# Decode attention and gated MLP on one core: eight megabytes of weights moved from SyncE's DMA queue to the head of ScalarE's

## The chip, the cores and the metric

The kernel runs on one core of one Trainium2 chip. The metric is the device time of one execution in microseconds (us). A core has five engines with an instruction stream each: TensorE (PE in the profile; its weight loads are PEld), VectorE (DVE), ScalarE (ACT), GpSimd (POOL) and SyncE (SP). Each stream runs strictly in its order; streams wait for each other on semaphores. DMAs are issued from SyncE's stream (SPq) and ScalarE's (ACTq); sixteen DMA engines move the data.

## What is computed

Two layers, each an attention block and a gated block with residuals, for 4 batches of one token (bf16). Both layers use the same weights and the same caches.

```python
def A(x, k_cache, v_cache, wq, wo):            # x: 4 x 1 x 512
    q = (x @ wq).reshape(B, Sq, 32, 128)       # 32 query heads, 8 key/value heads
    scores = einsum(q, k) * 128 ** -0.5        # caches: 4 x 8 x 4096 x 128
    return (softmax(scores) @ v) @ wo          # wo: 4096 x 512
def B(x, w_gate, w_up, w_down):                # 512 x 1792, 512 x 1792, 1792 x 512
    return (sigmoid(x @ w_gate) * (x @ w_up)) @ w_down
x = x + A(layernorm(x), ...);  x = x + B(layernorm(x), ...)
x = x + A(layernorm(x), ...);  x = x + B(layernorm(x), ...)
```

The caches and weights are 114.56 MB as they are read by this kernel (half of the heads' tiles are read a second time for the second layer).

## The kernel before

**Work.** A unit is one (batch, head group, layer), written `bhl`: unit 010 is batch 0, second group of four key/value heads, layer 0. The 16 units run in the order `000 010 100 011 110 200 001 111 ...` (UNITS, line 30). A unit of fresh tiles takes eight K tiles and eight V tiles of 512 KB. K tiles are transposed on VectorE (L723) and multiplied by the queries on TensorE (L731, `unit_scores`); softmax follows (`unit_probs`, L754 to L798), with its exponential and a copy on ScalarE; V tiles are multiplied by the probabilities (L815, `unit_values`), the result is copied by ScalarE (L827), selected (L832), scaled (L839) and multiplied by w_o (L850), which is added to x (L862). When both groups of a batch in layer 0 are done, `chain` runs its gated layer: mean and variance (L872 to L902), gate and up matmuls (L912), tanh on ScalarE (L932), product and transpose on VectorE (L937, L944), down matmuls (L954), x (L977) and the next layer's norm. Units with group 1 and layer 1 (011, 111, ...) use the tiles of group 1, layer 0, which stay in SBUF until then.

**Tiles.** K and V tiles live in a ring of 23 slots. A tile's load waits until the users of the slot's previous tile are done.

**Weights.** They have places of their own in SBUF and wait for nothing: w_q in two halves (wq0 for head group 0, wq1 for group 1; `load_wq`), w_o in four quarters (wo0 to wo3; `load_wo`), and w_gate, w_up, w_down (`load_glu`); all are issued at L519. Each has a semaphore of its own. One row that a DMA moves is 4,096 bytes of w_q, of a K or of a V tile, 3,584 of w_gate and w_up, 2,048 of w_down, 1,024 of w_o.

**What sets the order.** All loads are issued by SyncE in the order of the string LOADS (line 31):

```python
LOADS = "wq0 K0000 K0001 K0002 K0003 wq1 K0100 V0000 K0101 V0001 K0102 V0002 K0103 V0003
 wo0 wo1 wo2 wo3 K1000 K1001 K1002 K1003 V0100 V0101 V0102 V0103 wg wu wd V1000 ... V1003
 K1100 ... K1103 K2000 ... K2003 K0010 V1100 ..."          # each K or V word: two tiles
```

So the first 24 tiles are K of unit 000, then K of 010 and V of 000 in turn; then K of 100, V of 010, the weights of the gated layer, V of 100. `_Plan.schedule` plans all engines with a cost for each operation and a model of the loads, assigns slots, and writes each engine's order into `S.prog`. It also puts filler matmuls (L1105), which compute nothing that is used, where TensorE would stand idle by the plan; they keep their place in TensorE's order whatever happens on the chip. `emit` then writes each engine's stream from `S.prog`, with the waits. In the plan the tanh L932 waits for w_down as well as for its own inputs. TensorE's order around batch 0's gated layer is: the values of unit 010, its w_o, norm, gate, 13 fillers, up, 15 fillers, 4 fillers behind tanh, half of down, two value matmul groups of unit 100, the other half of down, the next norm, the queries of unit 011 mixed with more values of unit 100, the scores of unit 011.

In ScalarE's order the load of x (L447) is first; its first computation is `maskrs` (L695), ahead of it the table load, then the copy of the queries (L630).

The lines that emit the streams, and where the change is put:

```python
    S.schedule()
    with nc.Block() as block:
        for name, starter in (("sp", block.sync), ("act", block.scalar), ...):
            def body(e, name=name):
                S.emit(name, e, sems)
```

Of the kernel before, what the change touches and what calls it, by code (L numbers as in the profile page):

```python
# [350 lines left out]
def bass_interleave_layers__gqa_block_cached__glu_gated_glu__decode_kernel(nc, A_x, A_k, A_v, A_wq, A_wo, B_x, B_wg, B_wu, B_wd, out):  # L351
# [23 lines left out]
    S = _Plan(SLOTS)  # L375
# [3 lines left out]
    def sb(name, shape, dtype=dt.float32):  # L379
        return es.enter_context(nc.sbuf_tensor(name, list(shape), dtype))  # L380
# [8 lines left out]
    wg = sb("wg", [P, KD, F], bf)  # L389
    wu = sb("wu", [P, KD, F], bf)  # L390
    wd = sb("wd", [P, FB, D], bf)
# [713 lines left out]
    S.filler(lambda e: e.matmul(PT_ps[:, 0:256], lhsT=ident, rhs=flat_even[:, 0:256], start=True, stop=True), "PT")  # L1105

    S.schedule()
    with nc.Block() as block:
        for name, starter in (
            ("sp", block.sync), ("act", block.scalar), ("pe", block.tensor), ("dve", block.vector),  # L1110
            ("pool", block.gpsimd),
        ):
            def body(e, name=name):
                S.emit(name, e, sems)

            starter(body)
# [29 lines left out]
```

## Time and profile before

| what | value |
|---|---|
| runs shown | 314.67, 314.79 and 310.01 us, median 314.67 |
| profiled execution | 312.2 us; its span from first to last instruction 310.5 us |
| PE, PEld, DVE, ACT, POOL busy | 213.2, 114.2, 168.1, 60.8, 12.6 us |
| q1 (the loads) | 114.57 MB, 94.6% of sixteen engines' span |
| DMAs by SyncE | 96 K tiles, 96 V tiles, 2 of w_q, 4 of w_o, w_gate, w_up, w_down |
| TensorE's granted clock, mean | 0.899 |

How to read it: the slices of the page cut the span into 40 parts of 7.76 us; a digit is the busy share in tenths. A timeline line gives start, duration, engine, source line, operation, output <- inputs, shape and count, and in brackets the idle time just before it with what ended it. For SPq and ACTq lines the duration is that of the issuing instruction with its waits merged in; the landing of the data is shown as "us to landing" in the DMA view.

### The profile page before, as it was taken

The page shows a single profiled execution, that of the slowest core. Times are in us where ns is not written, and L with a number is a line of the kernel's source. Part 1 is how long each engine was busy: PE and PEld are TensorE (multiplying, and loading weights), DVE is VectorE, ACT ScalarE, POOL GpSimd, SP SyncE. Part 2 cuts the span into 40 slices and gives each one's busy share as a digit, 9 for nine tenths or more (in the row PEclk, how much of TensorE's full clock was granted, in tenths as well). Part 3 has the DMA queues.
Part 4 walks back from the last instruction along what each step waited for, and adds up shares of the span by engine and source line. Part 5 has one row for each costly group of instructions (what it writes and reads, how often), then busy time and mean ns, then how long its engine had stood idle before and what let it go on. Part 6 is the DMA issues. An engine that isn't in the chain of part 4 may idle for free.

```text
span 310.5 us, 7729 instructions
## 1 busy us (share of the span) xinstructions
PE 213.2 (69%) x3395; PEld 114.2 (37%) x3395; DVE 168.1 (54%) x314; ACT 60.8 (20%) x151; POOL 12.6 (4%) x44
## 2 busy tenths in 40 slices
PE   1344446577838976776996866885974757788694
PEld 1213114433425632243553422462431424534243
DVE  3675542483001699596217863736996952475112
ACT  0202002002101312021323120131330213231301
POOL 8000000000000000000000000000000000000001
PEclk9999999959995998599978877997897999979859
DMA  7999999999999999999999999799999999999900
GB/s 265 411 408 410 409 388 348 395 410 409 404 397 411 402 409 407 407 411 395 380 413 385 409 410 406 283 340 408 331 414 410 408 401 373 394 352 411 391 9 4
DMA packets 34931, 115.09 MB, mean 371 GB/s; under 512 B 3280, under 2 KB 7376, under 8 KB 34896
## 3 DMA queue, kind: packets, MB, share of 16 engines
q1 hardware_dynamic: 34832, 114.57, 94.6%
q8 instruction: 27, 0.44, 0.6%
q14 instruction: 8, 0.07, 0.1%
q10 hardware_dynamic: 64, 0.01, 0.0%
HBM read 114.56 MB, written 0.00 MB: 369 GB/s over the span
## 4 chain that ended last, share of the span: by engine, by line
DMA 57%; PE 25%; DVE 8%; SPq 4%; issue 3%; ACT 3%; POOL 1%; DVEq 0%; ACTq 0%
DMA ring<-in_A_k_cache_dram 20%; DMA ring<-in_A_v_cache_dram 17%; DMA wd<-in_B_w_down_dram 7%; PE S_ps L731 7%; DMA wq<-in_A_wq_dram 6%; DMA wo<-in_A_wo_dram 5%; PE O_ps L815 5%; DVE ring L723 4%; SPq L514 3%; PE M_ps L850 2%; PE Q_ps L651 2%; PE G_ps L954 1%; PE PT_ps L1105 1%; SPq L519 1%; PE PT_ps L779 1%
## 5 line engine op out<-in xcount | busy, mean ns | idle before, releaser
L723 DVE STREAM_TRANSPOSE ring<-ring 128x1024 int32<-128x1024 int32 x96 | 116.1, 1227 | 33.4 <-DMA ring<-in_A_k_cache_dram 32.6
L731 PE MATMUL S_ps<-ring,qz 128*32 128x512 bf16 x512 | 48.4, 505 | 32.7 <-DVE ring L723 26.0
L815 PE MATMUL O_ps<-ring,pt_sb 128*16 128x512 bf16 x512 | 45.4, 442 | 20.5 <-DMA ring<-in_A_v_cache_dram 17.5
L1105 PE MATMUL PT_ps<-even 128*128 128x256 bf16 x305 | 50.5, 305 | 8.9 <-ACT pp L932 4.3
L1105 PEld LDWEIGHTS PT_ps<-even 128*128 128x128 bf16 x305 | 29.1, 109 | 27.5 <-issue 9.8
L827 ACT ACTIVATE b<-O_ps 128x512 bf16<-128x512 f32 x32 | 19.1, 596 | 85.3 <-PE O_ps L815 81.8
L731 PEld LDWEIGHTS S_ps<-ring,qz 128*32 128x32 bf16 x512 | 13.9, 113 | 55.5 <-DVE ring L723 31.5
L768 ACT ACTIVATE pp<-S_ps,tr 128x512 bf16<-128x512 f32 x16 | 13.2, 828 | 50.4 <-DVE tr L761 48.5
L754 DVE TENSOR_REDUCE stat<-S_ps 128x1 f32<-128x512 f32 x16 | 11.1, 692 | 21.9 <-PE S_ps L731 21.8
L815 PEld LDWEIGHTS O_ps<-ring,pt_sb 128*16 128x16 bf16 x512 | 9.7, 89 | 32.8 <-issue 13.1
L850 PE MATMUL M_ps<-oT,wo 128*128 128x32 bf16 x512 | 15.8, 178 | 2.0 <-DMA wo<-in_A_wo_dram 1.6
L839 DVE TENSOR_TENSOR oT<-M_ps,rl 128x8 bf16<-128x8 f32 x32 | 4.9, 152 | 22.7 <-PE M_ps L832 22.7
L850 PEld LDWEIGHTS M_ps<-oT,wo 128*128 128x128 bf16 x512 | 14.1, 97 | 7.3 <-DVE oT L839 2.9
L902 POOL TENSOR_TENSOR stat<-stat 128x1 f32<-128x1 f32 x8 | 4.4, 545 | 256.2 <-ACT stat L898 256.2
L789 ACT ACTIVATE pt_sb<-PT_ps 128x512 bf16<-128x512 f32 x16 | 9.6, 597 | 17.6 <-PE PT_ps L779 17.6
L832 PE MATMUL M_ps<-sel_o,b 128*128 128x32 bf16 x128 | 8.7, 183 | 4.7 <-ACT b L827 4.6
L832 PEld LDWEIGHTS M_ps<-sel_o,b 128*128 128x128 bf16 x128 | 5.8, 101 | 16.1 <-ACT b L827 12.3
L937 DVE SCALAR_TENSOR_TENSOR b<-pp,U_ps 128x448 bf16<-128x448 f32 (+2 forms) x6 | 3.2, 538 | 14.5 <-ACT pp L932 12.9
L695 ACT ACTIVATE maskrs<-mask,stat 128x16 f32<-128x16 f32 x16 | 4.5, 304 | 28.5 <-DVE qz L700 26.5
L793 PE MATMUL M_ps<-sel_h,stat 128*128 128x16 f32 x32 | 6.7, 286 | 4.4 <-ACT pp L768 4.1
L774 DVE STREAM_TRANSPOSE pp<-pp 128x256 int32<-128x256 int32 x16 | 6.8, 426 | 5.2 <-ACT pp L768 5.2
L700 DVE TENSOR_TENSOR qz<-Q_ps,maskrs 128x256 bf16<-128x256 f32 x16 | 6.3, 394 | 6.0 <-PE Q_ps L690 6.0
(112 smaller groups left out, 162.6 us busy)
## 6 DMA issues: line engine op xcount, KB each, us to landing
ring<-in_A_k_cache_dram SPq DMA_DIRECT2D x96, 512.0 KB, 9.7
ring<-in_A_v_cache_dram SPq DMA_DIRECT2D x96, 512.0 KB, 10.2
wq<-in_A_wq_dram SPq DMA_DIRECT2D x2, 2048.0 KB, 13.8
wo<-in_A_wo_dram SPq DMA_DIRECT2D x4, 1024.0 KB, 14.7
wg<-in_B_w_gate_dram SPq DMA_DIRECT2D x1, 1792.0 KB, 16.1
wu<-in_B_w_up_dram SPq DMA_DIRECT2D x1, 1792.0 KB, 20.2
wd<-in_B_w_down_dram SPq DMA_DIRECT2D x1, 1792.0 KB, 22.7
xin<-in_A_x_dram ACTq DMA_DIRECT2D x1, 4.0 KB, 3.4
```

What stands on the lines that cost most here:

```text
L514: S.put("sp", lambda e: e.dma_start(ring[t.slot], src), dma="ring", load=t, size=0.524, cost=0.5)
L723: "dve", lambda e, t=t: e.transpose(ring[t.slot].bitcast(dt.int32), ring[t.slot].bitcast(dt.int32)),
L731: fns.append(lambda e, s=s, t=t, nn=nn, q=q: e.matmul(S_ps[qi][32 * s:32 * s + 32, :], lhsT=window(qi, s * NQ + nn, q), rhs=ring[t.slot].r ...
L754: dve(lambda e: e.tensor_reduce(ml[at], bank, AX.X, ALU.max, negate=True), keys(f"S{qi}", ss), keys("ml", ss), 0.7)
L768: lambda e: e.activation(p_sb[at].rearrange("p (t j r) -> p t r j", j=32, r=2), bank.rearrange("p (t r j) -> p t r j", r=2, j=32), ACTF.Ex ...
L774: dve(lambda e: e.transpose(pd[at].bitcast(dt.int32), p_sb[at].bitcast(dt.int32)), [own("P")], [own("P") + "d"], 0.4)
L789: "act", lambda e: e.activation(pt_sb[qi][:, cols], PT_ps[:, cols], ACTF.Copy),
L815: fns.append(lambda e, m=m, at=at, v=v, c=c, q=q: e.matmul(O_ps[m:m + 16, :], lhsT=pt[:, at:at + 16], rhs=ring[v.slot][:, c * 512:(c + 1) ...
L827: "act", lambda e: e.activation(b1[:], O_ps[:], ACTF.Copy),
L832: fns.append(lambda e, tt=tt: e.matmul(M_ps[:, 0:WIDE], lhsT=b1[:, tt * P:(tt + 1) * P], rhs=sel_o[:, tt, :].unsqueeze(1).broadcast_to([P, ...
L850: fns.append(lambda e, k=k, n=n, h0=h0: e.matmul(M_ps[:, k * WIDE:(k + 1) * WIDE], lhsT=wo[:, h0 + n, k * P:(k + 1) * P], rhs=oT[:, b, h0 ...
L1105: S.filler(lambda e: e.matmul(PT_ps[:, 0:256], lhsT=ident, rhs=flat_even[:, 0:256], start=True, stop=True), "PT")
```

## The change

After planning, the DMAs of wq1, w_gate, w_up, w_down and wo0 are taken out of SyncE's stream and put into ScalarE's, right behind the load of x and ahead of all its computation, in that order. Nothing else changes: the orders of the other engines, the slots of the ring, the fillers and all waits stay as planned. SyncE then issues wq0, the 24 tiles without wq1 among them, wo1 to wo3, K of 100, V of 010, V of 100 and so on without weights in between.

```diff
     S.schedule()
+
+    beside = [op for key in ("wq1", "wg", "wu", "wd", "wo0") for op in S.prog["sp"] if op.sem == key]
+    S.prog["sp"] = [op for op in S.prog["sp"] if op not in beside]
+    S.prog["act"][1:1] = beside
     with nc.Block() as block:
```

## The prediction

> **What bounds the kernel now.** I read the page's forty slices first, for the resource that is never idle.
>
> ```profile
> DVE  3675542483001699596217863736996952475112
> DMA  7999999999999999999999999799999999999900
> GB/s 265 411 408 410 409 388 348 395 410 409 404 397 411 402 409 407 407 411 395 380 413 385 409 410 406 283 340 408 331 414 410 408 401 373 394 352 411 391 9 4
> ```
>
> The DMA engines are full from the first slice to the 38th at about 410 GB/s; VectorE and TensorE are not. At that rate a 512 KB tile takes 512 KiB / 410 GB/s = 1.28 us. Time is lost only where the rate dips (slices 24 to 34) and in the tail. So the question is whether the change moves fewer bytes (no), moves them at another rate, or opens or closes a gap. The only early place where a weight ends a wait is batch 0's gated layer. The timeline of SyncE gives the issues around it:
>
> ```profile
> 66.03 0.33 SPq L514 DMA_DIRECT2D ring<-in_A_v_cache_dram  x1
> 66.40 0.43 SPq L519 DMA_DIRECT2D wg<-in_B_w_gate_dram  x1
> 66.88 2.54 SPq L519 DMA_DIRECT2D wu<-in_B_w_up_dram  x1
> 69.46 0.51 SPq L519 DMA_DIRECT2D wd<-in_B_w_down_dram  x1
> ...
> 95.94 0.33 SPq L514 DMA_DIRECT2D ring<-in_A_v_cache_dram  x1
> ```
>
> The first is the last V tile of unit 010; the DMA view gives it 12.0 us to landing, so it lands at 78.1. w_down takes 22.7 us and lands at 92.1. The timeline of all engines shows the layer running in the shadow of the weights:
>
> ```profile
> 78.12 0.61 PE L815 MATMUL O_ps<-ring,pt_sb 128*16 128x512 bf16 x8 [0.83 <-DMA ring<-in_A_v_cache_dram]
> 81.75 0.23 DVE L876 TENSOR_SCALAR small<-x,U_ps 128x4 bf16<-128x4 f32 x1 [0.55 <-PE U_ps L872]
> 82.67 0.74 PE L912 MATMUL G_ps<-wg,small 128*1 128x448 bf16 x12 [0.69 <-DMA wg<-in_B_w_gate_dram]
> 83.94 1.59 PE L1105 MATMUL PT_ps<-even 128*128 128x256 bf16 x13
> 87.11 0.93 PE L912 MATMUL U_ps<-wu,small 128*1 128x448 bf16 x16 [1.57 <-DMA wu<-in_B_w_up_dram]
> 87.97 1.81 PE L1105 MATMUL PT_ps<-even 128*128 128x256 bf16 x15
> 92.22 0.64 ACT L932 ACTIVATE pp<-G_ps,stat 128x448 f32<-128x448 f32 x1 [8.29 <-DMA wd<-in_B_w_down_dram]
> 92.91 0.61 PE L1105 MATMUL PT_ps<-even 128*128 128x256 bf16 x4 [3.13 <-ACT pp L932]
> 94.01 0.93 PE L954 MATMUL G_ps<-pp,wd 128*128 128x32 bf16 x28 [0.49 <-DVE pp L944]
> 94.86 1.03 PE L815 MATMUL O_ps<-ring,pt_sb 128*16 128x512 bf16 x8
> ```
>
> See that attention's end, norm, gate and up all run between 78 and 88 while weights land; only tanh onwards is left for after 92.1, and the down matmuls start at 94.0, 1.9 us behind the last weight. See also 13 + 15 + 4 L1105 filler matmuls, written into TensorE's order here to keep it busy during that wait. Behind them stand unit 100's value matmuls (94.86), which free the slots that SyncE waits for at 95.94.
>
> **Part 1: the bytes are kept, their order is not.** Nothing is added: 2.10 (w_q half) + 3 x 1.84 + 1.05 (w_o quarter) = 8.65 MB move to the second queue. SyncE's five issues go away; they cost it 0.43 to 2.54 us each, hidden since its tiles wait some 10 us in the queue (the page's medians, 9.7 and 10.2 us to landing). In the kernel before, 92.1 is when everything up to w_down has landed, with no dip except for w_o's short rows and instruction fetches. The same issues precede the last V tile of unit 010 in the new order, where it comes last instead of 14.0 us before the end. So that tile lands at 92.1 and not at 78.1, if the rate stays.
>
> How it gets there: the ScalarE queue has 3456 rows (512 each of w_q, w_gate, w_up; 896 of w_down; 1024 of w_o); SyncE's w_q half and first 23 tiles have 512 + 23 x 128 = 3456 too. With turns row by row both run until about 2.7 + 22.8 MB / 0.41 = 58, plus 1 to 2 us for short rows (357 GB/s between 45 and 58): 60 us. (2.7 is where 265 GB/s over the first 7.76 us puts the start.) Then tile 24, three w_o quarters (9 us), eight K and eight V tiles (20.5 us): 91 plus 1.4 to landing.
>
> The Trainium skill, "DMA: Bandwidth & Descriptors", section "Issuing engines are not separate DMA queues", speaks against the change: the queues share the same 16 engines, and a second issuer saves only issue time. By that rule the total stays at my sum; by the fastest row here (424 GB/s between 4 and 8 us) the 55.6 us of shared transfer would be 1.8 us shorter. No run here shows two busy queues yet.
>
> **Part 2: the early delay, costed at nothing.** ScalarE issues five DMAs ahead of its first table load (8.36). The queue accepts only so much: SyncE was stopped after some 8.4 MB were issued and 1.5 moved, about 1700 rows outstanding, and later with three w_o quarters, 3072 rows, outstanding. So ScalarE is free when 3456 - 3072 = 384 or 3456 - 1700 = 1756 rows are through: at 10 or 35 us. I take 26, between them, as its rows are of mixed size. Queued behind: maskrs L695 and the q copy L630, TensorE's L690, VectorE's L700, and six K transposes behind that. The cover is twofold. K tiles of unit 000 come at half rate, the last at 2.7 + (2 x 2.1 + 4.2 + 3.7) MB / 0.41 + 1.4 = 33.6 (19.1 before: issued at 5.00, 14.1 to landing). And the first slot is needed back by tile 24, which moves at 60; even from 35, two transposes (1.23 each) and 1.9 us of scores free it by 40. w_o's first quarter lands near 62 instead of in time for 48.85, but TensorE reaches it after tile 24 (62 to 63). With that cover gone, each us past 60 would be a us of idle queue.
>
> **Part 3: the layer now starts when it used to end.** From the landing at 78.07 the trace gives: norm done (L876) +3.9; gate matmuls without their wait for w_gate +4.0; L893 and the reciprocal root to +5.9; 13 fillers at 0.11 us from +5.3 to +6.7; up matmuls to +7.6; tanh +6.0 to +6.6, hidden; L937 must wait for up: +7.7 to +8.3; L944 to +8.8; meanwhile 15 + 4 fillers, 2.1 us from +7.6, hold TensorE until +9.7. Down starts at +9.7. Batch 1, with weights in place, is the check: last V tile used at 144.34, down at 153.53, +9.2 with other work between. 92.1 + 9.7 = 101.8 against 94.0: **7.8 us later** on TensorE. Without fillers it would be 8.8, so 6.9 us.
>
> **Part 4: what the queue feels.** SyncE's tiles wait for TensorE there. With the queue empty a tile takes 3.7 to 4.0 us from issue to landing:
>
> ```profile
> ring<-in_A_v_cache_dram SPq DMA_DIRECT2D x1, 512.0 KB, 3.7
> ring<-in_A_k_cache_dram SPq DMA_DIRECT2D x1, 512.0 KB, 4.0
> ```
>
> (issues at 199.65 and 216.90). The issues at 95.94, 99.12, 101.97 and 103.88 took 6.4, 5.8, 5.5 and 6.1 us, thus had 2.6, 2.0, 1.7 and 2.3 us in hand at 3.8. Each is released 7.8 us later; the third decides: 7.8 - 1.7 = **6.1 us of empty queue**. From there TensorE is 1.7 us further behind than the tiles. It wins that back at 127.91, where it idled 2.14 us for a V tile. All later waits keep their distance from the tiles, the 14.2 us of span after the last landing (282.12 + 14.2 = 296.3) included: nothing gives the 6.1 us back. Bounds: 6.9 - 1.7 = 5.2 without fillers in the way; 7.8 if slack is eaten by VectorE, which hardly pauses between 106 and 127; shared transfer faster by 1.8: 4.3.
>
> **Sum.** The profiled execution took 312.2 (span 310.5 + 1.7 around it): 312.2 + 6.1 = 318.3. The median of the runs, 314.67, lies 2.5 above it; I add to that: **320.8**. Own range 4.3 to 7.8: 319.0 to 322.5.
>
> **Rivals.** (a) *ScalarE is held until its last row has gone* (60 us). For it: SyncE's issue of w_o stood for 16.73 us. Against: it was still let go 9 us before w_o's last landing. Price: unit 000's first half scored at 65, tile 24 landing at 65 + 3.8 instead of 62.4: +6.4, in all 327.2. (b) *TensorE's clock is halved in the late layer*: it was granted 0.66 between 94 and 104. Fillers and matmuls on the path, some 4 us at full clock, cost up to 3 to 4 more: 324.3. (c) *SyncE's rows are preferred, weights trickle in last.* Then attention runs ahead, w_down still ends at 92.1, and the time is as before, 314.7. Against: the page's queue rows give instruction fetches 0.6% for 0.44 MB and q1 94.6% for 114.57 MB, 1.65 times as long per byte, near to even turns and no starving. (d) The other side: *two full queues raise the rate*, as one queue's gaps between rows are filled by the other. It decides from the point where the last V tile lands 6.1 us earlier: 49.5 us instead of 55.6 for the shared stretch, 461 GB/s. The fastest stretch seen is 424, and at 1.03 the engines' busy share already counts no gaps. At 480 it would give 312.7.
>
> **Numbers.** Forecast 0.55, (a) 0.10, (b) 0.10, (c) 0.13, (d) and part of it 0.12. Two per cent, about what a measurement of this kernel can tell from no change, is 6.3 us: the forecast sits on that line. Its 0.55 falls 0.25 slower, 0.30 within; (a), (b) slower; (c) within; (d) 0.06 faster, 0.06 within: faster 0.06, same 0.49, slower 0.45. The range leaves out half of (a) and (d): 314 to 326.
>
> **What would show it.** Right: ScalarE's first activation between 10 and 35; K tiles landing every 2.5 us early; last V tile of unit 010 at 92; tanh no longer waiting for w_down, down matmuls near 102 behind fillers; a dip in GB/s near 100 to 104; SyncE's wait for L815 near 104. Wrong: w_down landing after 85 (c); unit 010's last V tile before 87 (d); ScalarE idle to 60 (a); no dip at 100, or the dips between 199 and 277 shrinking to pay for it.

## The result, and the profile after

The changed kernel took 318.75 us (median; 317.74 to 319.44) against 312.75 for the kernel before it on the same chip: 6.0 us more, a ratio of 1.0266 [1.021, 1.0322]. The profiled execution took 319.44, its span 317.6. Ratios, here and below, compare undisturbed runs alone, so that they need not be the quotient of the medians beside them, and the profiles of E3, E4 and E8 below are of longer, disturbed executions and are read only up to 120 us.

The loads on ScalarE's queue are now a row of their own, q10. From part 3 and part 6 of the page (the last column is the median us from issue to landing):

```profile
q1 hardware_dynamic: 31296, 105.92, 85.9%
q10 hardware_dynamic: 3600, 8.66, 7.1%
...
wq<-in_A_wq_dram ACTq DMA_DIRECT2D x1, 2048.0 KB, 15.6
wg<-in_B_w_gate_dram ACTq DMA_DIRECT2D x1, 1792.0 KB, 24.2
wu<-in_B_w_up_dram ACTq DMA_DIRECT2D x1, 1792.0 KB, 32.8
wd<-in_B_w_down_dram ACTq DMA_DIRECT2D x1, 1792.0 KB, 45.5
```

Both queues spend the same engine time per byte (85.9% for 105.92 MB, 7.1% for 8.66 MB). ScalarE's timeline gives the other half, the issues and the first work behind them:

```profile
2.37 0.93 ACTq L519 DMA_DIRECT2D wu<-in_B_w_up_dram  x1
3.33 9.28 ACTq L519 DMA_DIRECT2D wd<-in_B_w_down_dram  x1
12.64 15.65 ACTq L519 DMA_DIRECT2D wo<-in_A_wo_dram  x1
28.38 1.28 ACT L695 ACT_TABLE_LOAD   x1 [28.38 <-issue]
```

w_down lands at 3.33 + 45.5 = 48.9 us instead of 92.1. So the layer has its weights early, but ScalarE begins at 28.38 instead of 8.36. The page's slices show where the time is lost:

```profile
DMA  7999999999995899998998999989999999999900
GB/s 262 413 409 407 402 400 396 380 362 407 409 409 212 325 386 413 409 409 310 374 404 305 400 409 409 408 314 388 398 411 411 408 404 379 407 288 413 408 36 3
```

A slice is 7.94 us. The 13th and 14th (95.3 to 111.2) stand at 212 and 325 GB/s where before stands at 402 to 411. Against 410 they lack 3.8 + 1.6 us. The timeline there:

```profile
92.28 0.61 PE L815 MATMUL O_ps<-ring,pt_sb 128*16 128x512 bf16 x8 [0.84 <-DMA ring<-in_A_v_cache_dram]
95.91 0.24 DVE L876 TENSOR_SCALAR small<-x,U_ps 128x4 bf16<-128x4 f32 x1 [0.55 <-PE U_ps L872]
96.20 0.74 PE L912 MATMUL G_ps<-wg,small 128*1 128x448 bf16 x12
97.47 1.59 PE L1105 MATMUL PT_ps<-even 128*128 128x256 bf16 x13
98.17 0.63 ACT L932 ACTIVATE pp<-G_ps,stat 128x448 f32<-128x448 f32 x1 [0.71 <-POOL stat L902]
99.00 0.93 PE L912 MATMUL U_ps<-wu,small 128*1 128x448 bf16 x16
99.86 2.25 PE L1105 MATMUL PT_ps<-even 128*128 128x256 bf16 x19
100.70 0.41 DVE L944 STREAM_TRANSPOSE pp<-b 128x224 int32<-128x224 int32 x1
101.94 0.85 PE L954 MATMUL G_ps<-pp,wd 128*128 128x32 bf16 x28
102.73 0.61 PE L815 MATMUL O_ps<-ring,pt_sb 128*16 128x512 bf16 x8
103.38 0.33 SPq L514 DMA_DIRECT2D ring<-in_A_v_cache_dram  x1
```

The same operations as before, in the same order, but with no wait for w_gate, w_up or w_down in brackets. The wait is now at the top: the last V tile of unit 010 lands at 92.23 (78.07 before). By then SyncE has issued seven more tiles, the last at 86.14, and they have landed at 101.09; no other slot is free until 103.38 (95.94 before), so that the queue runs empty. The window 100 to 104 (busy us of PE, PEld, DVE, ACT, POOL, then TensorE's granted clock, DMA share and GB/s):

```profile
100.00:104.00 4.00, 4.00 (x83) 3.33 (x81) 1.03 (x2) 0.00 (x0) 0.00 (x0) 1.00 0.03 10
```

and in the kernel before, where the rest of the tiles fills it:

```profile
100.00:104.00 4.00, 4.00 (x113) 2.92 (x114) 0.95 (x3) 1.17 (x5) 0.56 (x1) 0.90 1.03 408
```

The tile that SyncE asks for at its third wait (the fourth K tile of unit 110) lands at 113.49 instead of 107.45, **6.0 us** later: as much as the medians differ.

### The profile page after: what moved, and what is told of

Its sections match the earlier page's. It is cut to its first block, busy times and chain, and to the rows that moved or that the text cites. A ratio compares the mean times of both kernels' runs of the same rounds, so it can differ in the third digit from the quotient of the medians.

```text
span 317.6 us, 7729 instructions
## 1 busy us (share of the span) xinstructions
PE 211.3 (67%) x3395; PEld 114.0 (36%) x3395; DVE 166.8 (53%) x314; ACT 60.5 (19%) x151; POOL 12.6 (4%) x44
## 3 DMA queue, kind: packets, MB, share of 16 engines
q1 hardware_dynamic: 31296, 105.92, 85.9%
q10 hardware_dynamic: 3600, 8.66, 7.1%
## 4 chain that ended last, share of the span: by engine, by line
DMA 44%; PE 26%; DVE 12%; SPq 12%; ACT 3%; issue 3%; POOL 0%; DVEq 0%; ACTq 0%
DMA ring<-in_A_k_cache_dram 25%; DMA ring<-in_A_v_cache_dram 19%; SPq L514 11%; DVE ring L723 8%; PE O_ps L815 6%; PE S_ps L731 6%; PE PT_ps L1105 3%; PE M_ps L850 2%; PE G_ps L954 2%; PE Q_ps L651 1%; ACT b L827 1%; PE G_ps L912 1%; ACT pt_sb L789 1%; PE M_ps L832 1%; DVE stat L754 1%
## 5 line engine op out<-in xcount | busy, mean ns | idle before, releaser
L731 PE MATMUL S_ps<-ring,qz 128*32 128x512 bf16 x512 | 46.7, 488 | 29.0 <-DVE ring L723 23.8
L815 PE MATMUL O_ps<-ring,pt_sb 128*16 128x512 bf16 x512 | 44.5, 436 | 19.8 <-DMA ring<-in_A_v_cache_dram 17.0
L731 PEld LDWEIGHTS S_ps<-ring,qz 128*32 128x32 bf16 x512 | 13.5, 109 | 49.7 <-DVE ring L723 29.3
L690 PE MATMUL Q_ps<-q,even 128*128 128x16 bf16 x32 | 2.1, 177 | 17.1 <-ACT q L630 17.1
L779 PE MATMUL PT_ps<-pp,even 128*32 128x128 bf16 x256 | 7.2, 237 | 5.0 <-DVE oT L839 3.2
## 6 DMA issues: line engine op xcount, KB each, us to landing
wd<-in_B_w_down_dram ACTq DMA_DIRECT2D x1, 1792.0 KB, 45.5
```

Source lines behind the costliest of these rows:

```text
L731: fns.append(lambda e, s=s, t=t, nn=nn, q=q: e.matmul(S_ps[qi][32 * s:32 * s + 32, :], lhsT=window(qi, s * NQ + nn, q), rhs=ring[t.slot].r ...
L779: fns.append(lambda e, s=s, a=a: e.matmul(PT_ps[32 * a:32 * a + 32, s * P:(s + 1) * P], lhsT=ident[at, 32 * s:32 * s + 32], rhs=spread[:, ...
L815: fns.append(lambda e, m=m, at=at, v=v, c=c, q=q: e.matmul(O_ps[m:m + 16, :], lhsT=pt[:, at:at + 16], rhs=ring[v.slot][:, c * 512:(c + 1) ...
```

## The experiments

Three theories. **Late values** (mine): the order alone delays the last V tile of unit 010; the layer starts there and frees slots only at its end. **Held ScalarE**: the 20 us that its first work is delayed come back later. **Two queues**: two full queues cost or bring rate. Ratios are against the kernel before on the same chip.

**E1. The two parts that are not the layer's: half of w_q and a quarter of w_o on ScalarE.** As the changed kernel, with

```diff
-    beside = [op for key in ("wq1", "wg", "wu", "wd", "wo0") for op in S.prog["sp"] if op.sem == key]
+    beside = [op for key in ("wq1", "wo0") for op in S.prog["sp"] if op.sem == key]
```

> Only the w_q half and the w_o quarter go to ScalarE; w_gate, w_up and w_down stay in SyncE's order. Late values (the loss comes from the last V tile of unit 010 landing at 92 instead of 78): both weights preceded that tile anyway, so it lands at 78 again, the down matmuls of batch 0 start at 94, time as before, within 1 us. Held ScalarE (the loss comes from its hold of 28 us): the hold falls to some 5 us or less, a loss of under 1.5 us. Two queues (the loss comes from the sharing itself): 3.1 of the 8.65 MB are shared, a loss near 2 us.

313.51 against 313.85, 0.9992 [0.9952, 1.0031]. In its PE timeline values and down start as before:

```profile
78.57 0.61 PE L815 MATMUL O_ps<-ring,pt_sb 128*16 128x512 bf16 x8 [0.51 <-DMA ring<-in_A_v_cache_dram]
94.11 0.93 PE L954 MATMUL G_ps<-pp,wd 128*128 128x32 bf16 x28 [0.34 <-DVE pp L944]
```

A second queue by itself, with 3.1 of the 8.65 MB, costs and brings nothing that can be measured; the loss hangs on the gated layer's three weights.

**E2. The order without the second queue.** From the kernel before: the three weights stay on SyncE and are issued behind w_o.

```diff
     S.schedule()
+    early = [op for key in ("wg", "wu", "wd") for op in S.prog["sp"] if op.sem == key]
+    S.prog["sp"] = [op for op in S.prog["sp"] if op not in early]
+    at = [op.sem for op in S.prog["sp"]].index("wo3") + 1
+    S.prog["sp"][at:at] = early
```

> No DMA moves to ScalarE at all; w_gate, w_up and w_down are only moved ahead in SyncE's own order, in front of unit 100's K tiles and unit 010's V tiles. Late values: the last V tile of unit 010 lands at 92 and the time is 6 us over before, as in the changed kernel. Held ScalarE and two queues: neither exists here, time as before.

318.05, 1.0133 [1.0045, 1.0221]: 4.2 us over before by the ratio, where I had put 6. ScalarE starts at 8.44, yet the chain is that of the changed kernel within 0.3 us, and the window 100 to 104 is as empty:

```profile
91.99 0.61 PE L815 MATMUL O_ps<-ring,pt_sb 128*16 128x512 bf16 x8 [0.82 <-DMA ring<-in_A_v_cache_dram]
99.56 2.25 PE L1105 MATMUL PT_ps<-even 128*128 128x256 bf16 x19
101.65 0.85 PE L954 MATMUL G_ps<-pp,wd 128*128 128x32 bf16 x28
```

```profile
100.00:104.00 4.00, 3.84 (x81) 3.09 (x78) 0.91 (x3) 0.00 (x0) 0.00 (x0) 1.00 0.02 8
```

The third-wait tile lands at 113.34. Neither a second queue nor a held ScalarE is needed for the loss.

**E3. Both queues, ScalarE not held.** The first three DMAs stay ahead; w_down and w_o's quarter go behind ScalarE's first nine operations.

```diff
-    S.prog["act"][1:1] = beside
+    S.prog["act"][9:9] = beside[3:]
+    S.prog["act"][1:1] = beside[:3]
```

> The changed kernel, but w_down and the w_o quarter are issued by ScalarE only behind its first softmax copy, so that its first activation is not held: it starts near 8 to 9 us instead of 28.4. Late values: the last V tile still lands at 92, time as the changed kernel, 6 us over before. Held ScalarE: the loss goes, time as before. Two queues: as the changed kernel.

320.38, 1.0159 [1.0072, 1.0245]. ScalarE's timeline, then TensorE's:

```profile
2.36 1.13 ACTq L519 DMA_DIRECT2D wu<-in_B_w_up_dram  x1
8.34 1.28 ACT L695 ACT_TABLE_LOAD   x1 [8.34 <-POOL stat L610]
```

```profile
92.00 1.03 PE L815 MATMUL O_ps<-ring,pt_sb 128*16 128x512 bf16 x8 [0.15 <-DMA ring<-in_A_v_cache_dram]
102.07 0.85 PE L954 MATMUL G_ps<-pp,wd 128*128 128x32 bf16 x28
```

The table load is back at 8.34 and nothing is gained: held ScalarE falls as a cause.

**E4. The changed kernel without the 32 fillers between gate and down** (13 ahead of up, 19 ahead of down).

```diff
+    pe = S.prog["pe"]
+    gate = [n for n, op in enumerate(pe) if op.stage == "g0"][0]
+    down = [n for n, op in enumerate(pe) if op.stage == "d0"][0]
+    S.prog["pe"] = [op for n, op in enumerate(pe) if not (gate < n < down and op.fns == [S.fill])]
```

> The changed kernel without the 32 filler matmuls between gate and down of batch 0 (they compute nothing that is used). Late values with fillers on the path: down starts 8.8 instead of 9.7 us after the last V tile, SyncE's wait ends 0.9 us earlier, time 0.9 us under the changed kernel (5.1 over before). If the fillers are hidden: no difference from the changed kernel, down still at 101.9.

316.86, 1.0117 [1.0046, 1.0188]. Down starts 7.8 us behind the last V tile (92.61 to 100.38) instead of 9.7; the first wait ends at 102.26 and the third-wait tile lands at 112.97, 1.1 and 0.5 us earlier. Whether the time follows is below the noise here, so R3 repeats it.

**E5. A dose: gate and up alone moved.** The list is `("wg", "wu")`.

> Only w_gate and w_up go to ScalarE; w_down stays behind unit 010's V tiles in SyncE's order. Late values predicts a threshold, not a share: the last V tile lands 5.05 us (w_down's transfer) before 92.1, at 87.1; the down matmuls start at 87.1 + 9.7 = 96.8 instead of 94.0; of those 2.8 us the queue has 1.7 in hand: 1.1 us over before. Held ScalarE: 3.7 of the 8.65 MB, hold below 5 us, time as before. Two queues: in proportion, 0.43 x 6 = 2.5 us over before.

```profile
87.57 1.00 PE L815 MATMUL O_ps<-ring,pt_sb 128*16 128x512 bf16 x8
97.63 0.85 PE L954 MATMUL G_ps<-pp,wd 128*128 128x32 bf16 x28
```

The V tile lands at 87.53, down starts 10.1 us behind it, 3.6 later than before; the slots' slack eats half, and the third-wait tile lands 1.7 us late. 314.63 against 312.88: 1.75 us, 1.0048 [1.0001, 1.0094]. My value, 1.1, lies nearer than the 2.5 of a loss in proportion to the bytes, but the interval (0 to 2.9 us) holds both: what tells them apart is the timeline, where two thirds of the bytes bring 28% of the delay at the third wait.

**E6 and E7. The same 28 more fillers behind the up matmuls, in the changed kernel (E6) and in the one before (E7).** If the stretch is on the path in one and covered in the other, they cost 3.1 us in the one only.

```diff
+    pe = S.prog["pe"]
+    up = [n for n, op in enumerate(pe) if op.stage == "g0"][-1] + 1
+    S.prog["pe"] = pe[:up] + [pe[up]] * 28 + pe[up:]
```

> The changed kernel with 28 more filler matmuls (0.11 us each, 3.1 us) behind batch 0's up matmuls. Late values: TensorE's order is the path there now, no wait covers them: down starts 3.1 us later, at 105, SyncE's first wait ends near 106.5, and the time is 3 us over the changed kernel, 9 over before. If something else sets the end: as the changed kernel.

> The kernel before with the same 28 fillers in the same place. Late values: the wait for w_down covers them (TensorE idled 3.1 us there until tanh), down still starts at 94.0, time as before. If fillers cost by themselves (clock, instruction fetches): 1 to 3 us over before.

TensorE in E7: 47 fillers end before w_down's data allow down to begin, at 94.02 as without them (94.01).

```profile
88.33 5.31 PE L1105 MATMUL PT_ps<-even 128*128 128x256 bf16 x47
94.02 0.87 PE L954 MATMUL G_ps<-pp,wd 128*128 128x32 bf16 x28 [0.38 <-DVE pp L944]
```

In E6 down moves from 101.94 to 104.90 and the third-wait tile from 113.49 to 117.18. In time E6 took 319.78, 1.0225 [1.015, 1.03], only 1.0 above the changed kernel's earlier median, measured on another occasion, and with a ratio below its 1.0266: the 3 us do not show there. E7 took 311.03, 0.9949 [0.9911, 0.9987]: not a cost but a small gain, which neither theory gives. R4 sets E6 beside the changed kernel.

**E8. All engines planned anew.** From the kernel before, with `wg wu wd` in LOADS moved from behind V0103 to behind wo3, so that the planner knows of the order.

> SyncE alone, w_gate, w_up and w_down ahead of unit 100's K tiles, but now in the load order that the planner is given, so that all engines are planned for it: fewer fillers around the layer, and unit 100's first value matmuls stand ahead of the down matmuls. Late values: the last V tile still lands at 92, but the path behind it loses its 2 us of fillers and the first slot wait no longer hangs on the layer: 2 to 5 us over before, below the 6 of the changed kernel. If the loss is only the stale order: time as before.

The planner puts values of unit 100 ahead of down, and the slots come free in time:

```profile
92.04 0.84 PE L815 MATMUL O_ps<-ring,pt_sb 128*16 128x512 bf16 x8 [0.74 <-DMA ring<-in_A_v_cache_dram]
...
97.25 0.61 PE L815 MATMUL O_ps<-ring,pt_sb 128*16 128x512 bf16 x8
...
101.14 1.53 PE L954 MATMUL G_ps<-pp,wd 128*128 128x32 bf16 x55
```

SyncE's issue is at 96.03 (95.94 before), the third-wait tile at 107.31 (107.45). The gap is not gone, it has moved. SyncE's next long wait, 6.9 us, ends at 111.00, when the scores of unit 011 (L731) release a slot; they begin at 108.63 instead of 102.71, behind the next norm, whose L872 stands at 103.16 instead of 97.08. SyncE's waits (us in total, times, longest) and the windows:

```profile
SPq L514 <- PE S_ps L731: 7.7, 2, 6.9
```

```profile
104.00:108.00 4.00, 3.56 (x108) 3.17 (x108) 3.96 (x6) 1.31 (x7) 0.55 (x1) 0.74 1.01 404
108.00:112.00 4.00, 3.37 (x32) 1.27 (x36) 3.23 (x5) 0.31 (x1) 0.00 (x0) 0.50 0.46 171
112.00:116.00 4.00, 2.83 (x35) 1.23 (x30) 3.18 (x9) 0.87 (x2) 0.00 (x0) 0.90 0.96 352
```

At 408 GB/s the last two lack 2.32 + 0.55 = 2.9 us. I had put 2 to 5 us over before; the time is inconclusive: ten runs from 312.4 to 322.4, median 316.88, 1.0048 [0.9983, 1.0113], which is 1.5 us over before, between 0.5 under and 3.5 over.

**R1 to R4. Four kernels on one chip:** the changed kernel, and E2, E4 and E6 again.

> The changed kernel once more, beside the next three on one chip, since earlier medians lie 1 to 2 us apart by themselves. Late values: 6 us over before.

> SyncE alone with w_gate, w_up and w_down ahead, once more. Late values: as the changed kernel of this call, within 1 us. Two queues or held ScalarE add a part: 2 us under the changed kernel (a first look gave 4.2 over before against 6.0).

> The changed kernel without the 32 fillers, once more. The trace of the first look had down 7.8 us behind the last V tile instead of 9.7, and the first slot wait ended 1.1 us earlier. If the delay at that place is carried to the end: 1 to 2 us under the changed kernel. If later gaps give part of it back: less than 1 us under.

> The changed kernel with 28 more fillers, once more. In the first look the tiles near 117 landed 3.7 us later than in the changed kernel, but the median was only 1.0 us longer. If the delay is carried to the end: 3 us over the changed kernel. If later gaps give part of it back: 1 to 2 us over.

| kernel | last V tile lands | down starts | first wait ends | third-wait tile lands | median us | ratio [95%] |
|---|---|---|---|---|---|---|
| before (on this chip: 312.19) | 78.07 | 94.01 | 95.94 | 107.45 | 312.19 | 1 |
| R1 changed | 92.19 | 101.89 | 103.33 | 113.81 | 317.04 | 1.0169 [1.0104, 1.0233] |
| R2 order alone | 92.41 | 102.11 | 103.55 | 115.08 | 319.37 | 1.0177 [1.007, 1.0284] |
| R3 without fillers | 92.38 | 100.50 | 101.93 | 113.56 | 316.87 | 1.0176 [1.0115, 1.0237] |
| R4 28 more fillers | 92.31 | 105.06 | 106.50 | 117.06 | 320.24 | 1.028 [1.0224, 1.0337] |

(The columns of landings for "before" are those of its profile shown earlier.) R2 and R1 have nearly the same ratio, so the order alone is enough for the loss. R2's interval is wide: the times would leave room for a part of up to a per cent, either way, for the second queue. The tiles leave less: that of the second wait lands at 110.82 in R1 and at 111.10 in R2. R4's fillers on TensorE,

```profile
99.92 5.30 PE L1105 MATMUL PT_ps<-even 128*128 128x256 bf16 x47
105.06 0.85 PE L954 MATMUL G_ps<-pp,wd 128*128 128x32 bf16 x28
```

put 3.2 us on down, 3.2 on the first wait and 3.2 on the median over R1, though the two intervals still overlap by 0.001. With E7, the same work is free where w_down's transfer covers it and, in the timelines of E6 and R4, costs its full length where it does not; in the medians that rests on R4 beside R1. R3,

```profile
97.86 0.93 PE L912 MATMUL U_ps<-wu,small 128*1 128x448 bf16 x16
100.50 0.85 PE L954 MATMUL G_ps<-pp,wd 128*128 128x32 bf16 x28 [1.71 <-issue]
```

frees the first slot 1.4 us sooner and gains 0.2, nothing that can be measured: its third-wait tile lands only 0.25 us before R1's. That tile and the one ahead of it landed 2.21 and 2.13 us behind the tile before them instead of some 1.28, and the transfer fell to 98 and 33 GB/s from 107.25 to 107.75 and to 131, 131 and 115 from 111.5 to 112.25. What slowed it was not tried and stays open.

## Why the prediction was right, point by point

**The order (parts 1 and 3): right.** The last V tile landed at 92.23 for 92.1, down began 9.71 us later for 9.7. E2 and R2 show that the order alone does this, E3 that a held ScalarE is not needed either with both queues, E5 how much remains with part of it. Rate: 408 GB/s from 14 to 34 us and 397 from 50 to 60 with both queues busy, so rival (d), a raised rate, is out, and (c) too, as w_down came first. The Trainium skill, "DMA: Bandwidth & Descriptors", section "Issuing engines are not separate DMA queues", has it that DMAs of different issuers share the same 16 engines; E1 and R1 beside R2 agree.

**The early delay (part 2): right, costed at nothing.** ScalarE was free at 28.38 for 26; the last K tile of unit 000 landed at 31.8 for 33.6, tile 24 at 62.65 for 62.4, w_o's quarter at 61.1 for 62. Rival (a) needed a hold to 60.

**The clock: rival (b) is out.** TensorE was granted 1.00 from 92 to 104. In the late layer it had been granted 0.62 before:

```profile
92.00:100.00 8.00, 6.28 (x103) 3.73 (x104) 1.50 (x5) 1.79 (x5) 0.00 (x0) 0.62 1.03 409
```

and after

```profile
92.00:100.00 8.00, 7.36 (x106) 4.18 (x107) 0.57 (x4) 1.97 (x6) 0.55 (x1) 1.00 0.94 372
```

**What the queue feels (part 4): 6.0 for 6.1, by luck.** Two terms were wrong and cancel. "Each is released 7.8 us later" held for none: the three waits end 7.44, 6.54 and 6.47 us later (103.38, 105.66, 108.44 for 95.94, 99.12, 101.97). The clock has a part in it: the eight value matmuls between the halves of down took 1.03 us before and 0.61 now. And 3.8 us from issue to landing held for none: the tiles took 3.3, 5.3 and 5.0 us.

```profile
ring<-in_A_v_cache_dram SPq DMA_DIRECT2D x1, 512.0 KB, 3.3
```

```profile
ring<-in_A_k_cache_dram SPq DMA_DIRECT2D x1, 512.0 KB, 5.3
```

```profile
ring<-in_A_k_cache_dram SPq DMA_DIRECT2D x1, 512.0 KB, 5.0
```

So at the third wait 6.5 + 5.0 - 5.5 = 6.0 instead of 7.8 + 3.8 - 5.5 = 6.1.

Nor does the third wait decide. By the prediction's terms the tiles of the three waits come 5.2, 5.8 and 6.1 us late; they came 4.3, 6.06 and 6.04 late (106.64, 110.95 and 113.49). The third follows the tile ahead of it after 1.26 us, as in a full queue. In windows of half a microsecond nothing is transferred from 100.5 to 104, and 344 to 434 GB/s from 105 to 112: the engines stand still ahead of the first wait alone, and only its tile goes into an empty queue. Why the tile of the second wait took 5.3 us, so that the delay grows from 4.3 to 6.06, was not tried; R1 (4.7 to 5.9) and R2 (4.75 to 6.2) show the same step.

**Without fillers (part 3): mis-sized.** "Without fillers it would be 8.8" counted the 19 behind up and forgot the 13 ahead of it: 7.8 (E4) and 8.1 (R3). That moves the lower bound, not the forecast.

**"Nothing gives the 6.1 us back": right within 1.3 us in the medians.** Tile by tile it holds less well: against before, tiles of the changed kernel's profile land 7.7 us later at tile 80, 9.5 at 100, 6.4 at 160 and 8.3 at the last; in R1's, 6.7, 6.8, 5.5 and 6.2. Each run has gaps of its own behind the first 48 tiles.

**The total: 318.75 for 320.8.** The difference was predicted as 6.1 and measured as 6.0 in this comparison and 4.85 in R1's. The 2 us that the total is off are the base: 314.67 was the median of three runs, 312.75 with a fourth. The chances leaned a little to within 2% (0.49 against 0.45 for slower); 1.0266 [1.021, 1.0322] lies beyond that line, and 1.0169 [1.0104, 1.0233] on either side of it.

## What to carry to other kernels

When the DMA engines are full, a load that is moved forward pushes another back by its own length: ask which tile becomes the late one, what work hangs on it, and whether the work that the moved load used to cover has any cover left. Here w_down's transfer was the cover under which attention's end, norm, gate and up ran, and the price is the uncovered length less the slack of the slots behind it, not the bytes moved. Extra work put on the suspected stretch, the same in both kernels, is a cheap test of whether it is covered: 28 fillers left the down matmuls where they were before, and put them 3.2 us later after the change.

## What the runs showed of the hardware that was not expected

- Two busy queues take turns by rows, not by bytes. SyncE's tiles of 4 KB rows came every 2.5 us beside rows of 4 and 3.5 KB, every 2.05 us beside w_down's 2 KB rows and every 1.70 us beside w_o's 1 KB rows. One tile alone takes 1.28 us; alone w_down landed 5.05 us behind w_up before (issue and time to landing: 66.88 + 20.2 and 69.46 + 22.7) and three quarters of w_o took 9. As an estimate, a row of the other queue for each of its own makes 1.28 + 5.05 / 7 = 2.00 beside w_down (896 rows, seven times a tile's 128) and 1.28 + 3.0 / 8 = 1.65 beside w_o's quarter (1024 rows): short rows get fewer bytes.
- TensorE's clock in the late layer. Before, TensorE idled 3.13 us until tanh and was granted 0.62 from 92 to 100. E7 is the same kernel with 28 more fillers in that wait, and there the same stretch was granted 1.00 (the number ahead of the DMA share):

```profile
92.00:100.00 8.00, 7.09 (x162) 5.35 (x159) 1.66 (x6) 2.40 (x8) 0.55 (x1) 1.00 1.03 408
```

  The busy share alone does not set it: R3 was granted 0.93 with 6.29 of these 8 us busy, the kernel before 0.62 with 6.28. Nor is it fixed for a kernel: E4 and R3, which are one kernel, were granted 0.62 and 1.00 from 100 to 104.
- The time of one kernel goes with the mean granted clock, loosely. Of the 25 runs of the kernel before beside E5 to E8, the five granted 0.911 or more took 310.55 to 312.86 us and the seven granted 0.878 or less 314.13 to 317.55, but one at 0.879 took 311.74. Which follows from which is not shown.
- E7's extra fillers left the kernel before 0.5% faster, 0.9949 [0.9911, 0.9987], the only one whose interval lies below 1. Its ten runs were granted 0.896 to 0.918 on the mean, the 25 of the kernel before 0.858 to 0.921; whether the clock is the cause is open.
